# The order of the pieces in a program for linear attention and a feed-forward layer

## The chip, the cores and the metric

One core of one Trainium2 chip. The metric is the device time of one execution in microseconds (us). The kernel uses TensorE (PE in the profile), VectorE (DVE), ScalarE (ACT) and GpSimd (POOL) for arithmetic, and SyncE (SP) for most transfers. Each engine works through its own queue in the order in which the program gave its instructions out; an instruction that waits holds up all that stand behind it on that engine.

## The reference

```python
# q, k, v: (8, 8, 576, 64); w_in: (512, 2048); w_out: (2048, 512); all fp32
q_s = softmax(q, axis=-1)            # over the 64 of a head
k_s = softmax(k, axis=2)             # over the 576 positions
kv  = einsum('bhsd,bhse->bhde', k_s, v)   # per head k_s^T v, 64 x 64
x   = (q_s @ kv), heads side by side     # 4608 tokens x 512
g   = softplus(x @ w_in)             # 4608 x 2048
out = g @ w_out                      # 4608 x 512
```

q, k, v and w_in are drawn with large factors, so the products are done to nearly fp32 accuracy: each operand is split in a high part and a low rest, and a product is three matmuls (high x high, low x high, high x low).

## The kernel before, in words

The 4608 tokens are nine tiles of 512. The first three are done one by one: `U` makes one of 16 blocks of 128 of the hidden layer (12 matmuls, lines 595 to 597), `A` applies softplus on ScalarE (line 604), `G` or `H` splits the result in high and low parts (ScalarE line 610, VectorE line 613), `O` or `I` adds its product with a block of w_out (12 matmuls, lines 637 to 639), `F` stores the finished tile (line 653). The other six tiles are done as three pairs, with a scheme of seven products instead of eight on 2 x 2 blocks: `X` makes sums of the inputs (lines 679 to 686), `C` is a product of the first layer (lines 722 to 724, with evictions at 734 to 756), `t` a difference (803), `e` splits an operand in a high part (ScalarE, `e...0`, line 816) and a low part (VectorE, `e...1`, line 819), `d` is a product of the second layer (836 to 838), and `o` gathers and stores the pair's output: evictions on ScalarE (856) or VectorE (859), `flip` a transposition (873), `store` four stores on GpSimd's queue (881), and for the last block `addp`, `turnp`, `takep`, `storep` (889 to 905). In `C`, `d`, `e`, `t` and `o` the first number is the pair.

The scheme needs sums of weight blocks. `D` keeps a split weight in DRAM (line 220), `Y` and `y` make the sums (252 to 293) and their step 8 stores them in DRAM (265, 293), `R` and `r` fetch blocks and sums back (224 to 241, 790). Attention is made between the products: `n` loads keys and values (314 and 318, after GpSimd has cleared part of the buffer, 310 to 313), `k` makes kv of a head pair (336 to 413, products on PE at 387), `L` loads and `q` normalizes the queries (432, 453 to 502), and `x` multiplies them with kv (519 to 547, VectorE's low part at 529, products at 535 to 537). `l`, `T`, `M`, `S`, `J`, `P`, `Q` load, unpack, scale and split weights; `w` issues small matmuls that only keep PE running at the start (1038).

Nothing plans at run time. The string ORDER lists the tokens, and a loop at the end gives each token to `do`, which calls the piece of code that issues its instructions:

```python
        order = ORDER.split()
        for token in order:
            do(token)
```

Waits follow from the data: an instruction waits for its inputs, and for the buffer that it writes to be free. The pools have few buffers, so a load waits for the last reader of its buffer. A token `S` issues something only if its weight isn't in the set `signed` that `M` fills:

```python
                if at[0] not in signed:
                    sign_w(at[0], on(at, (nc.vector, nc.gpsimd, nc.scalar)))
```

Of the kernel before, what the change touches and what calls it, by code (L numbers as in the profile page):

```python
# [1096 lines left out]
```

## Time and profile before

| | before |
|---|---|
| time, median of 3 runs | 814.21 us (813.40 to 814.42) |
| profiled execution, span | 811.1 us; no time of its own is listed beside the span |
| median of the runs less that span | 3.1 us |
| PE busy | 800.8 us (99%) |
| VectorE, ScalarE, GpSimd busy | 625.9, 536.3, 115.1 us |
| transfers | 193.75 MB, mean 239 GB/s |

The span is the time from the first to the last recorded instruction; what lies around it is in the time of a run only. "SPq" is SyncE's queue of transfers, "PEld" the loading of weights into PE, which runs beside the matmuls. A matmul's record lasts longer than the distance to the next one, since matmuls are pipelined; the distance is the cost. A transfer has two times: that of its issue in a queue, and the time until it has landed.

### The profile page before, as it was taken

The page shows a single profiled execution, that of the slowest core. Times are in us where ns is not written, and L with a number is a line of the kernel's source. Part 1 is how long each engine was busy: PE and PEld are TensorE (multiplying, and loading weights), DVE is VectorE, ACT ScalarE, POOL GpSimd, SP SyncE. Part 2 cuts the span into 40 slices and gives each one's busy share as a digit, 9 for nine tenths or more (in the row PEclk, how much of TensorE's full clock was granted, in tenths as well). Part 3 has the DMA queues.
Part 4 walks back from the last instruction along what each step waited for, and adds up shares of the span by engine and source line. Part 5 has one row for each costly group of instructions (what it writes and reads, how often), then busy time and mean ns, then how long its engine had stood idle before and what let it go on. Part 6 is the DMA issues. An engine that isn't in the chain of part 4 may idle for free.

```text
span 811.1 us, 12147 instructions
## 1 busy us (share of the span) xinstructions
PE 800.8 (99%) x4244; PEld 656.6 (81%) x4244; DVE 625.9 (77%) x1027; ACT 536.3 (66%) x868; POOL 115.1 (14%) x219
## 2 busy tenths in 40 slices
...
GB/s 340 373 273 182 59 39 274 267 176 385 401 279 257 328 337 343 340 372 253 139 324 237 186 115 265 275 270 93 280 201 197 178 261 198 175 156 322 211 126 70
DMA packets 114493, 193.75 MB, mean 239 GB/s; under 512 B 8000, under 2 KB 90176, under 8 KB 104192
## 3 DMA queue, kind: packets, MB, share of 16 engines
...
## 4 chain that ended last, share of the span: by engine, by line
PE 92%; DVE 3%; issue 2%; DMA 2%; SPq 1%; ACT 0%; POOL 0%; DVEq 0%; ACTq 0%; POOLq 0%
PE po L722 6%; PE po L838 6%; PE po L836 6%; PE po L837 6%; PE po L724 6%; PE po L723 6%; PE ph L595 5%; PE po L637 5%; PE ph L597 5%; PE ph L596 5%; PE po L638 5%; PE po L639 5%; PE ph L722 3%; PE ph L724 3%; PE ph L723 3%; PE ph L836 3%
## 5 line engine op out<-in xcount | busy, mean ns | idle before, releaser
L881 POOL DMA_DIRECT2D out<-w x92 | 59.3, 653 | 305.7 <-DVE w L873 304.4
L816 ACT CAST g_hi<-w 128x512 fp32r<-128x512 f32 x74 | 46.2, 624 | 31.1 <-PE ph L837 8.0
L595 PE MATMUL ph<-x,w 128*128 128x512 f32 x164 | 65.3, 398 | 1.1 <-DMA w<-kept 1.1
L637 PE MATMUL po<-w,g_hi 128*128 128x512 f32 x164 | 64.5, 394 | 0.0
L596 PE MATMUL ph<-x,w 128*128 128x512 f32 x164 | 64.0, 390 | 0.0
L597 PE MATMUL ph<-x,w 128*128 128x512 f32 x164 | 64.0, 390 | 0.0
L639 PE MATMUL po<-w,g_lo 128*128 128x512 f32 x164 | 64.0, 390 | 0.0
L638 PE MATMUL po<-w,g_hi 128*128 128x512 f32 x164 | 63.9, 390 | 0.0
L819 DVE TENSOR_TENSOR g_lo<-w,g_hi 128x512 fp32r<-128x512 f32 x74 | 51.0, 690 | 16.0 <-ACT g_hi L816 12.6
L803 DVE TENSOR_TENSOR w<-w,w 128x512 f32<-128x512 f32 x72 | 49.2, 686 | 5.3 <-ACT w L756 5.2
L752 ACT ACTIVATE w<-w 128x512 f32<-128x512 f32 x48 | 30.1, 632 | 34.8 <-DVE w L745 18.9
L745 DVE TENSOR_TENSOR w<-po,w 128x512 f32<-128x512 f32 x24 | 16.6, 690 | 46.9 <-PE po L724 46.3
L816 ACT CAST w<-w 128x512 fp32r<-128x512 f32 x52 | 32.2, 623 | 25.1 <-DVE w L819 8.1
L604 ACT ACTIVATE g<-ph 128x512 f32<-128x512 f32 x48 | 28.6, 599 | 29.8 <-PE ph L597 26.7
L722 PE MATMUL po<-w,x 128*128 128x512 f32 x112 | 44.1, 394 | 0.0
L724 PE MATMUL po<-w,x 128*128 128x512 f32 x112 | 43.7, 390 | 0.0
L723 PE MATMUL po<-w,x 128*128 128x512 f32 x112 | 43.7, 390 | 0.0
L610 ACT CAST g_hi<-g 128x512 fp32r<-128x512 f32 x46 | 28.6, 621 | 21.2 <-PE po L638 20.7
L613 DVE TENSOR_TENSOR g_lo<-g,g_hi 128x512 fp32r<-128x512 f32 x46 | 31.4, 683 | 12.6 <-ACT g_hi L610 12.4
L339 POOL PARTITION_ALL_REDUCE mx<-mx x20 | 17.2, 860 | 160.6 <-DVE mx L336 133.0
L336 DVE TENSOR_REDUCE mx<-kvt 128x128 f32<-128x640 f32 x28 | 36.9, 1319 | 2.5 <-DMA kvt<-in_kv_tail 2.5
L819 DVE TENSOR_TENSOR w<-w,w 128x512 fp32r<-128x512 f32 x52 | 35.6, 689 | 3.1 <-ACT w L816 1.0
...
## 6 DMA issues: line engine op xcount, KB each, us to landing
...
```

What stands on the lines that cost most here:

```text
L595: nc.tensor.matmul(ph, lhsT=w_hi, rhs=x_hi, start=h == 0, stop=False)
L596: nc.tensor.matmul(ph, lhsT=w_lo, rhs=x_hi, start=False, stop=False)
L597: nc.tensor.matmul(ph, lhsT=w_hi, rhs=x_lo, start=False, stop=h == HP - 1)
L637: nc.tensor.matmul(po, lhsT=g_hi[:, ms], rhs=w_hi, start=j == 0, stop=False)
L638: nc.tensor.matmul(po, lhsT=g_hi[:, ms], rhs=w_lo, start=False, stop=False)
L639: nc.tensor.matmul(po, lhsT=g_lo[:, ms], rhs=w_hi, start=False, stop=j == NJ - 1)
L722: nc.tensor.matmul(ph, lhsT=w_hi, rhs=x_hi, start=c == 0 and i in (0, 4), stop=False, **more)
L723: nc.tensor.matmul(ph, lhsT=w_lo, rhs=x_hi, start=False, stop=False, **more)
L724: nc.tensor.matmul(ph, lhsT=w_hi, rhs=x_lo, start=False, stop=c == 1, **more)
L816: nc.scalar.copy(ring[p, i, s][0], right_of(p, i, s))
L819: engine.tensor_tensor(out=lo, in0=right_of(p, i, s), in1=hi.bitcast(F32), op=ALU.subtract)
L836: nc.tensor.matmul(bank, lhsT=w_hi, rhs=hi, start=begin, stop=False, **more)
```

## The change

ORDER is replaced by another list. It holds the same tokens, 2420 of the 2432; the 12 that are left out are `S` tokens of weights that are in `signed` at that point in the order before. No other line is changed. Of the diff, which replaces the whole list, five stretches are shown: the start, the end of the sum `Y1` of weight blocks, the stretch with the fetches of weight blocks 3 and 4, a stretch of the last pair, and the end. In each the removed lines are the old order from one token to another, and the added lines the new one; they are broken at other places here than in the file.

```diff
 ORDER = """
-    w0.20 b0 b1 q0.0 n k0.0.1 n q0.1 n n q0.2 q0.3 q0.4.1 l0 q0.5 l1 k0.0.2 k0.1.1 l2 k0.1.2 k0.0.3 k0.2.1
-    k0.0.4 k0.0.5 q0.6
+    w0.20 b0 q0.0 b1 q0.1 n n n n q0.2 q0.3 q0.5 q0.4.1 q0.6
...
-    Y1.7 k3.0.5 L4 H1.13.1 Y6.0 O28 k3.1.5 q3.0 A30 Y6.1 R0.1 q3.1 U31 H1.14.0 Y7.0 q3.12 H1.14.1 Y1.8
+    Y1.7 k3.1.4
...
-    k3.0.6 H1.15.0 y0.0 k3.1.6 q3.5 n H1.15.1 U32 k3.0.7 y0.1 k3.1.7 y0.2 q3.6 q3.7 R0.2 k3.0.8 O30 q3.8 A32
-    k3.0.9 y0.3 Y4.2 k3.1.8 n k3.2.0 U33 q3.13 k3.1.9 H2.0.0 q3.9 R0.3 H2.0.1 O31 k3.2.4 A33 q3.10 y1.0
-    k3.3.0 U34 F1.0 F1.1 q3.11 F1.2 F1.3 R0.4 k3.3.4 H2.1.0 U35 A34 H2.1.1 k3.2.5 y1.1 q4.0 O32 k3.3.5 q4.1
-    A35 y0.4 y1.2 y0.5 y1.3 q4.12 y2.0 k3.2.6 R0.5 y1.4 k3.3.6 H2.2.0 q4.2 n k3.2.7 q4.3 y0.6 O33 k3.2.8
-    H2.2.1 k3.3.7 k3.2.9 k3.3.8 q4.4 U36
+    k3.0.6 k3.1.5 n x2.3.5 k3.0.7 k3.0.8 k3.1.6 k3.1.7 k3.0.9 k3.1.8 k3.1.9 U32 q3.6 q4.1 q3.8 H1.15.0 O30 n
+    q3.5 q3.7 H1.15.1 O31 A32 U33 H2.0.0 q4.0 U34 Y1.8 H2.0.1 q3.13 R0.3 A33 H2.1.0 R0.4 F1.0 F1.1 Y7.1 y1.0
+    y0.0 F1.2 F1.3 O32 R0.5 U35 Y4.2 Y6.1 Y6.3 k3.2.0 k3.3.0 y0.1 y0.2 A34 y0.3 q3.9 y0.4 k3.3.4 y0.5 q4.12
+    k3.2.4 k3.2.5 k3.2.6 q3.10 H2.1.1 q4.2 q3.11 q4.3 k3.3.5 k3.3.6 k3.2.7 A35 H2.2.0 n U36
...
-    d2.2.7 e2.6.3.1 e2.4.2.0 e2.4.2.1 d2.4.0 t2.4.6 e2.4.3.0 r2.13 o2.c11.0 e2.4.3.1 d2.4.1 t2.4.7 e2.4.4.0
-    o2.c11.1 e2.4.4.1 d2.4.2 o2.flip.0.0 e2.4.5.0 e2.4.5.1 o2.store.0.0 d2.4.3
+    d2.2.7 e2.4.1.0 d2.4.0 r2.9 e2.4.1.1 d2.4.1 e2.4.3.0 e2.4.3.1 o1.store.1.1 e2.4.2.0 o2.c11.1 o2.flip.0.1
+    o2.c11.0 e2.4.2.1 d2.4.2 e2.4.4.0 e2.4.6.0 e2.4.4.1 t2.4.2 e2.6.0.0 e2.6.0.1 e2.4.5.0 d2.4.3
...
-    d2.5.7 e2.6.6.0 e2.6.6.1 d2.6.0.0 o2.c12.0 e2.6.7.0 d2.6.1.0 e2.6.7.1 d2.6.2.0 o2.c12.1 o2.flip.3.0
-    d2.6.3.0 d2.6.4.0 o2.flip.3.1 o2.store.3.0 d2.6.5.0 d2.6.6.0 d2.6.7.0 o2.store.3.1 d2.6.0.1 o2.c21.0
-    d2.6.1.1 o2.flip.2.0 d2.6.2.1 d2.6.3.1 o2.store.2.0 d2.6.4.1 d2.6.5.1 d2.6.6.1 d2.6.7.1 o2.addp.0
-    o2.addp.1 o2.turnp.0 o2.turnp.1 o2.takep.0 o2.turnp.2 o2.takep.1 o2.turnp.3 o2.takep.2 o2.storep.0
-    o2.takep.3 o2.storep.1
+    d2.5.7 o2.flip.0.0 e2.6.2.0 o2.store.0.0 e2.6.2.1 e2.6.1.1 d2.6.1.0 d2.6.0.1 e2.6.6.0 e2.6.6.1
+    o2.flip.1.1 d2.6.1.1 o2.store.1.1 o2.c12.1 d2.6.2.0 d2.6.2.1 o2.c12.0 o2.flip.3.0 r2.13 d2.6.3.0 d2.6.4.0
+    o2.store.3.0 o2.flip.3.1 e2.6.5.1 d2.6.5.0 o2.store.3.1 d2.6.6.0 e2.6.7.0 e2.6.7.1 d2.6.7.0 o2.c21.0
+    o2.flip.2.0 d2.6.3.1 d2.6.4.1 d2.6.5.1 d2.6.6.1 d2.6.7.1 o2.addp.0 o2.turnp.0 o2.takep.0 o2.addp.1
+    o2.turnp.1 o2.takep.1 o2.storep.0 o2.turnp.2 o2.takep.2 o2.turnp.3 o2.store.2.0 o2.takep.3 o2.storep.1
 """
```
## Rows read from the trace of the kernel before

**Rows 1.** The page's busy time: engine, us (share of the span) x instructions.
```profile
PE 800.8 (99%) x4244; PEld 656.6 (81%) x4244; DVE 625.9 (77%) x1027; ACT 536.3 (66%) x868; POOL 115.1 (14%) x219
```

**Rows 2.** The chain of work that ended last, shares of the span by engine.
```profile
PE 92%; DVE 3%; issue 2%; DMA 2%; SPq 1%; ACT 0%; POOL 0%; DVEq 0%; ACTq 0%; POOLq 0%
```

**Rows 3.** Who PE waited for: us in total, times, longest.
```profile
PE ph L595 <- DMA w<-kept: 1.1, 1, 1.1
...
PE att L535 <- DVE q_lo L529: 0.7, 1, 0.7
...
PE att L387 <- issue: 0.4, 1, 0.4
```

**Rows 4.** Windows: stretch, length, busy time of the engines, PEclk, DMA share, GB/s.
```profile
480.00:500.00 20.00, 19.87 (x88) 16.01 (x86) 17.43 (x29) 10.45 (x18) 5.47 (x8) 1.00 0.48 160
560.00:580.00 20.00, 20.00 (x90) 16.55 (x89) 15.71 (x25) 15.79 (x31) 0.00 (x0) 1.00 0.55 165
```

**Rows 5.** The chain of waits in order of time, around U35: start, us, what.
```profile
224.82 8.94 DMA w<-kept
...
233.89 0.47 PE ph L595
```

**Rows 6.** Timeline of SyncE's DMA queue, 208 to 232: start, duration, line, transfer.
```profile
208.98 0.76 SPq L265 DMA_DIRECT2D sums<-w  x1
...
218.57 0.55 SPq L314 DMA_DIRECT2D kvt<-in_kv  x1
219.17 1.73 SPq L318 DMA_DIRECT2D kvt<-in_kv_tail  x1
...
221.65 0.54 SPq L314 DMA_DIRECT2D kvt<-in_kv  x1
222.23 2.55 SPq L318 DMA_DIRECT2D kvt<-in_kv_tail  x1
224.82 0.85 SPq L224 DMA_DIRECT2D w<-kept  x1
...
231.14 1.43 SPq L224 DMA_DIRECT2D w<-kept  x1
```

**Rows 7.** Timeline, the products of two key/value units on PE.
```profile
217.60 1.39 PE L387 MATMUL att<-kvt 128*64 128x65 f32 x40
```

**Rows 8.** Line 265, the stores of the summed weights.
```profile
DMA to landing us min/median/max: 5.6/8.6/12.8
```

**Rows 9.** Line 224, the fetches of weight blocks.
```profile
DMA to landing us min/median/max: 4.7/8.3/10.6
```

**Rows 10.** Timeline around the short stall at 491.
```profile
489.80 0.62 ACT L816 CAST w<-w 128x512 fp32r<-128x512 f32 x1
...
490.70 0.69 DVE L819 TENSOR_TENSOR w<-w,w 128x512 fp32r<-128x512 f32 x1
490.92 0.39 PE L837 MATMUL po<-w,spare 128*128 128x512 f32 x1
...
491.44 0.51 PE L838 MATMUL po<-w,spare 128*128 128x512 f32 x1
```

**Rows 11.** The page's costliest groups: busy us, mean ns of one, idle before.
```profile
L816 ACT CAST g_hi<-w 128x512 fp32r<-128x512 f32 x74 | 46.2, 624 | 31.1 <-PE ph L837 8.0
...
L819 DVE TENSOR_TENSOR g_lo<-w,g_hi 128x512 fp32r<-128x512 f32 x74 | 51.0, 690 | 16.0 <-ACT g_hi L816 12.6
```

**Rows 12.** Groups by line: the eviction of line 856.
```profile
L856 ACT ACTIVATE w<-po 128x512 f32<-128x512 f32 x17 | 10.1, 592 | 8.3 <-PE po L838 8.1
```

**Rows 13.** The chain of waits at the start.
```profile
23.84 1.76 PE ph L1038 x14
25.60 3.44 PE po L558 x8
```

**Rows 14.** Timeline of GpSimd near the end.
```profile
797.94 7.69 POOL L881 DMA_DIRECT2D out<-w  x12 [5.00 <-DVE w L873]
```

**Rows 15.** Timeline of SyncE's DMA queue at the end.
```profile
807.49 1.21 SPq L904 DMA_DIRECT2D out<-w  x2
```

**Rows 16.** Line 881, GpSimd's stores of the result.
```profile
DMA to landing us min/median/max: 2.2/2.9/6.5
```

More of the change, by code (lines that the diff above doesn't have):

```diff
@@ new lines @@
+    w0.20 b0 q0.0 b1 q0.1 n n n n q0.2 q0.3 q0.5 q0.4.1 q0.6 k0.0.1 k0.0.2 k0.1.1 k0.0.3 k0.1.2 k0.2.1 k0.2.2
+    k0.1.3 w5.5 k0.2.3 k0.0.4 k0.0.5 k0.1.4 k0.1.5 k0.2.4 k0.2.5 k0.3.1 k0.3.2 k0.0.6 l0 T0 M0.1 w1.6 l1 l2 l3 n
+    l4 q0.8 k0.3.3 q0.7 k0.1.6 k0.3.4 z1 T1 M1.1 k0.3.5 k0.0.7 k0.0.8 q0.12 q0.13 q0.9 w2.3 q0.11.1 w3.2 w4.2
+    q0.10 T2 k0.1.7 k0.1.8 k0.2.6 k0.3.6 k0.2.7 k0.2.8 x0.1.0 x0.1.1 T3 x0.0.0 x0.0.1 x0.2.0 x0.2.1 n k0.3.7
+    k0.3.8 x0.3.0 x0.1.2 l5.6.7.8.9 J0 x0.3.1 x0.0.2 B0 L1 k1.0.0 k1.0.1 B1 x0.2.2 B2 x0.3.2 k1.0.2 M3 S3.1 J1
@@ new lines @@
+    k1.0.3 k1.0.4 B3 k1.1.0 x0.1.3 x0.1.4 T4 M4.1 U0 M2.1 J2 k1.0.5 J3 U1 A0 P2 Q2 k1.1.1 x0.2.3 k1.1.2 x0.0.3
+    A1 x0.0.4 x0.3.3 x0.3.4 k1.0.6 k1.0.7 T5 P3 x0.2.4 Q3 T7 O0 U2 U3 M5 A2 J4 P4 Q4 G2 k1.1.3 A3 O1 O2 S5.1 J5
+    k1.1.4 M7.1 q1.0 q1.1 q1.2 T6 q1.3 P5 M6.1 J7 W1 Q5.1 U4 k1.1.5 G3 T8 J6 M8.1 J8 A4 U5 A5 k1.1.6 P6 Q6 G4 D6
+    q1.4 T9 M9 O3 O4 P7 Q7 U6 U7 G5 k1.1.7 z0 k1.0.8 O5 P8 Q8 S9 J9 T12 A6 U8 T10 G6 O6 M10 S10 J10 T11 D7
+    k1.1.8 P9 Q9 k1.2.0 T15 A7 P10 k1.0.9 k1.2.1 G7 D5 O7 k1.3.0 k1.1.9 k1.3.1 k1.2.2 T13 k1.2.3 k1.2.4 U9 A8
@@ new lines @@
+    Q10 U10 q1.6 G8 T14 O8 M12.1 M11.1 J11 k1.2.5 J12 W2 P11 W0 k1.3.2 k1.3.3 Q11 M13.1 k1.3.4 A9 A10 k1.2.6
+    k1.2.7 P12 Q12 J13 G9 M15.1 J15 U11 U12 q1.8 O9 k1.3.5 k1.3.6 M14.1 G10 O10 J14 q1.5 q1.7 P13 Q13 A11 A12
+    G11 O11 U13 k1.2.8 k1.2.9 k1.3.7 G12 P14 Q14 P15 q1.9 q1.10 x1.0.0 Q15.1 U14 q1.11 A13 k1.3.8 k1.3.9 x1.1.0
+    O12 P0 W3 x1.0.1 x1.0.2 x1.0.3 G13 A14 G14 x1.0.4 x1.0.5 O13 x1.1.1 x1.1.2 x1.1.3 U15 x1.2.0 x1.2.1 x1.2.2
+    x1.1.4 x1.2.3 O14 Q0.1 x1.1.5 P1 Q1.1 D1 x1.3.0 x1.3.1 x1.3.2 x1.3.3 L2 A15 x1.2.4 x1.2.5 D15 x1.3.4 x1.3.5
@@ new lines @@
+    H1.7.0 H1.7.1 n A24 H1.8.0 U25 k2.3.6 O23 D10 D12 k3.0.0 Y4.0 H1.8.1 L3 Y4.1 D13 x2.0.1 U26 x2.0.2 Y2.3
+    x2.0.3 A25 H1.9.0 q3.1 Y3.2 Y3.3 H1.9.1 Y3.4 k2.3.7 A26 Y2.4 k2.3.8 O24 O25 Y2.5 Y2.6 k2.3.9 Y3.5 Y3.6 Y2.7
+    x2.1.0 x2.1.1 H1.10.0 Y1.0 Y1.2 Y1.3 x2.0.4 U27 A27 H1.10.1 D8 x2.0.5 x2.2.0 k3.0.4 k3.0.5 x2.1.2 U28 A28
+    Y1.4 n x2.1.3 x2.1.4 H1.11.0 x2.2.1 Y1.5 Y1.6 q3.0 U29 q3.12 x2.1.5 x2.3.0 Y2.8 R0.0 D9 O26 H1.12.0 Y0.5
+    H1.11.1 O27 x2.2.2 x2.2.3 Y3.7 A29 Y3.8 L4 R0.1 H1.13.0 Y6.0 U30 H1.12.1 O28 A30 Y6.2 k3.1.0 U31 Y7.0 Y7.2
@@ new lines @@
+    H1.13.1 q3.2 q3.3 q3.4 x2.3.1 Y0.6 x2.2.4 Y0.7 Y0.8 A31 x2.3.2 H1.14.0 x2.3.3 R0.2 O29 Y1.7 k3.1.4 H1.14.1
+    x2.3.4 x2.2.5 k3.0.6 k3.1.5 n x2.3.5 k3.0.7 k3.0.8 k3.1.6 k3.1.7 k3.0.9 k3.1.8 k3.1.9 U32 q3.6 q4.1 q3.8
+    H1.15.0 O30 n q3.5 q3.7 H1.15.1 O31 A32 U33 H2.0.0 q4.0 U34 Y1.8 H2.0.1 q3.13 R0.3 A33 H2.1.0 R0.4 F1.0 F1.1
+    Y7.1 y1.0 y0.0 F1.2 F1.3 O32 R0.5 U35 Y4.2 Y6.1 Y6.3 k3.2.0 k3.3.0 y0.1 y0.2 A34 y0.3 q3.9 y0.4 k3.3.4 y0.5
+    q4.12 k3.2.4 k3.2.5 k3.2.6 q3.10 H2.1.1 q4.2 q3.11 q4.3 k3.3.5 k3.3.6 k3.2.7 A35 H2.2.0 n U36 Y7.3 q4.4
@@ new lines @@
+    k3.2.8 k3.2.9 x3.0.0 y0.6 n q4.5 O33 U37 H2.2.1 O34 R0.6 R0.7 k3.3.7 y1.1 H2.3.0 H2.3.1 k4.0.0 q4.6 q4.8
+    R2.0 x3.0.1 x3.0.2 x3.0.3 k3.3.8 k3.3.9 x3.1.0 k4.1.0 A36 H2.4.0 O35 y2.0 x3.1.1 x3.1.2 x3.1.3 Y4.3 Y4.4
+    x3.0.6 A37 x3.2.0 Y7.4 R0.8 U38 H2.5.0 x3.2.1 q4.7 H2.4.1 x3.2.2 x3.2.3 k4.0.4 q4.13 Y5.1 k4.0.5 y0.7 Y7.5
+    y0.8 q4.9 O36 x3.1.6 x3.3.0 H2.5.1 x3.2.6 y2.1 k4.0.6 y1.2 y1.3 x3.3.1 x3.3.2 A38 H2.6.0 Y4.5 q4.11 k4.1.4
+    k4.1.5 O37 n x3.3.3 x3.3.6 U39 A39 H2.7.0 R0.9 k4.0.7 R0.10 y1.4 y3.1 Y6.4 q4.10 k4.1.6 k4.0.8 k4.2.0 y3.0
@@ new lines @@
+    U40 U41 y1.5 y1.6 k4.2.4 H2.6.1 H2.7.1 O38 O39 Y7.6 y4.0 y3.2 Y6.5 y1.7 k4.1.7 A40 n y4.1 Y5.0 Y4.6 Y6.6
+    H2.8.0 H2.8.1 O40 k4.1.8 Y6.7 A41 H2.9.0 k4.2.5 y2.2 k4.3.0 k4.0.9 H2.9.1 Y4.7 k4.3.4 k4.3.5 Y7.7 U42 A42
+    k4.1.9 y1.8 y4.2 Y5.2 k4.2.6 k4.2.7 y2.3 R0.11 k4.2.8 y5.0 Y5.3 Y5.4 k4.3.6 k4.3.7 k4.3.8 Y4.8 X0.1.hB11
+    k4.2.9 y3.3 x4.0.0 x4.0.1 O41 y3.4 y3.5 Y5.5 R0.12 H2.10.0 Y5.6 U43 R0.13 A43 Y7.8 x4.0.2 Y6.8 H2.10.1
+    k4.3.9 x4.1.0 x4.0.3 x4.1.1 x4.1.2 U44 x4.1.3 Y5.7 H2.11.0 x4.0.6 x4.2.0 Y5.8 X0.0.hB11 X0.0.lB11 x4.2.1
@@ new lines @@
+    x4.2.2 x4.1.6 A44 O42 H2.12.0 x4.3.0 x4.2.3 x4.3.1 H2.11.1 O43 X0.0.T1 X0.0.hT1 R0.14 R0.15 y5.1 R3.1.0
+    x4.3.2 x4.2.6 X0.0.hB22 X0.0.T3 x4.3.3 X0.0.lB22 X0.0.T2 y4.3 n n R3.0.0 y3.6 H2.12.1 x4.3.6 X0.0.hB21
+    X0.0.lB21 y2.4 X0.1.lB11 X0.1.T1 X0.1.T3 X0.1.hT1 y4.4 X0.1.hB22 X0.1.lB22 X0.1.T2 y2.5 U45 U46 A45 A46
+    X0.1.hB21 X0.1.lB21 X0.1.hT3 O44 X0.0.T4 H2.13.0 U47 H2.14.0 X0.1.hT2 X0.1.T4 y4.5 y5.2 y4.6 R2.1 X0.0.hT2
+    H2.13.1 H2.14.1 y6.0 R4.1.0 y3.7 O45 y3.8 y6.1 y7.1 y5.3 y5.4 y7.0 X0.0.hT3 X0.1.hT4 X0.1.lT4 R4.3.0 A47
@@ new lines @@
+    C0.0.0 C0.0.7 y4.7 y6.2 y2.6 X0.0.hT4 H2.15.0 I2.14.1 I2.14.0 H2.15.1 X0.0.lT4 C0.0.2 y4.8 I2.15.1 y5.5 y5.6
+    I2.15.0 X0.1.lT1 X0.0.lT1 L5 F2.0 X0.1.lT2 X0.0.lT2 C0.0.1 C0.0.8 C0.1.0 F2.1 y5.7 y6.3 y6.4 y6.5 C0.0.3
+    R4.0.0 R3.2.0 C0.1.7 C0.1.2 C0.1.1 C0.0.10 X0.0.lT3 F2.2 C0.0.5 y7.2 F2.3 X0.1.lT3 C0.0.4 C0.0.11 q5.1 y2.7
+    C0.1.8 k5.0.0 y7.3 y7.4 k5.0.4 y7.5 C0.1.3 C0.0.9 e0.0.0.0 C0.2.0 e0.0.0.1 C0.0.6 C0.1.10 k5.1.0 y5.8
+    C0.0.14 C0.1.4 C0.1.11 C0.2.7 y7.6 C0.2.2 R2.2 C0.1.5 C0.2.1 R3.3.0 C0.1.6 C0.2.9 k5.1.4 C0.1.9 k5.0.5 q5.0
@@ new lines @@
+    k5.3.7 C0.3.6 C0.3.15 C0.4.5 R2.6 C0.5.7 C0.5.2 C0.6.0 k5.2.8 k5.2.9 x5.0.0 x5.0.1 R4.7.0 C0.4.14 C0.6.7
+    C0.5.1 C0.5.8 k5.3.8 x5.0.2 x5.0.3 C0.4.11 C0.4.6 y7.7 C0.0.16 C0.5.3 q6.0 k5.3.9 x5.0.6 t0.1.0 C0.5.10
+    x5.1.0 x5.1.1 q6.1 q6.12 x5.1.2 C0.2.12 C0.4.12 C0.5.4 k6.0.0 C0.5.5 C0.5.11 k6.1.0 x5.1.3 R3.7.0 C0.5.14
+    C0.5.9 C0.6.1 C0.6.8 x5.2.0 x5.2.1 x5.1.6 R4.5.0 C0.5.6 C0.7.0 C0.6.3 x5.2.2 x5.2.3 y7.8 C0.5.15 k6.0.4
+    C0.6.2 k6.0.5 x5.2.6 C0.6.10 k6.1.4 C0.7.7 x5.3.0 k6.0.6 R4.6.0 R2.7 C0.7.1 t0.1.3 C0.4.15 x5.3.1 e0.0.1.0
@@ new lines @@
+    e0.0.1.1 k6.1.5 x5.3.2 C0.6.4 e0.0.2.0 x5.3.3 e0.0.3.0 C0.6.11 C0.6.12 t0.1.4 C0.2.16 n k6.0.7 k6.0.8 k6.0.9
+    k6.2.0 C0.6.5 C0.6.14 r0.0 e0.0.2.1 C0.7.4 C0.6.6 C0.6.15 k6.2.4 x5.3.6 k6.1.6 k6.1.7 n C0.7.8 t0.1.1
+    C0.1.12 C0.6.9 k6.1.8 k6.1.9 X1.0.hB11 C0.7.2 C0.7.9 C0.7.3 C0.7.10 q6.2 q6.3 d0.0.0 d0.0.1 r0.1 q6.4 q6.6
+    d0.0.2 X1.1.hB11 e0.0.6.0 C0.7.11 e0.0.3.1 k6.3.0 C0.7.6 e0.0.4.0 e0.0.5.0 r0.4 C0.7.5 r0.2 t0.1.5 q6.5
+    k6.2.5 k6.3.4 k6.3.5 C0.7.15 C0.7.16 e0.0.4.1 q6.7 d0.0.3 q6.8 k6.2.6 C0.7.12 k6.2.7 k6.3.6 e0.0.5.1
@@ new lines @@
+    e0.1.2.1 t0.3.2 n d0.1.2 t0.2.7 d0.1.3 r0.9 e0.1.4.0 t0.2.5 t0.3.0 C0.5.16 X1.0.hB21 e0.1.6.0 t0.3.4
+    e0.1.4.1 d0.1.4 e0.1.5.0 e0.2.0.0 e0.1.5.1 e0.1.6.1 e0.1.7.0 X1.1.lB11 o0.v.1 d0.1.5 d0.1.6 e0.1.7.1 d0.1.7
+    e0.2.1.0 e0.2.0.1 C0.3.16 d0.2.0 X1.1.lB21 t0.3.5 n t0.3.7 e0.2.2.0 e0.2.2.1 e0.2.3.0 e0.2.1.1 d0.2.1 t0.4.3
+    e0.2.3.1 C0.4.16 e0.2.4.0 e0.2.5.0 e0.2.4.1 o0.u.1 d0.2.2 d0.2.3 e0.2.7.0 q6.9 q6.10 k6.3.9 e0.2.5.1 t0.4.7
+    C0.6.16 x6.0.0 e0.2.6.0 e0.2.6.1 x6.0.1 e0.2.7.1 d0.2.4 x6.1.0 e0.4.0.0 d0.2.5 d0.2.6 e0.4.1.0 e0.4.0.1
@@ new lines @@
+    e0.4.1.1 x6.0.2 e0.4.2.0 t0.4.4 o0.u.0 e0.4.2.1 t0.3.6 d0.2.7 e0.4.3.0 r0.8 q6.11 d0.4.0 e0.4.3.1 x6.0.3
+    x6.0.6 x6.1.1 x6.1.2 d0.4.1 d0.4.2 e0.4.4.0 e0.4.4.1 x6.2.0 X1.0.lB11 x6.1.3 e0.4.5.0 e0.4.5.1 x6.2.1 x6.1.6
+    X1.1.T1 r0.13 d0.4.3 e0.4.7.0 d0.4.4 e0.4.6.0 e0.4.6.1 e0.5.0.0 d0.4.5 r0.12 o0.v.0 x6.2.2 x6.2.3 r0.10
+    x6.2.6 x6.3.0 x6.3.1 d0.4.6 e0.5.2.0 t0.4.0 e0.4.7.1 d0.4.7 e0.5.1.0 X1.0.T1 x6.3.2 e0.5.0.1 o0.c22.1 d0.5.0
+    e0.5.1.1 d0.5.1 e0.5.4.0 e0.5.5.0 e0.5.3.0 X1.0.T3 X1.0.hB22 e0.5.2.1 o0.c22.0 e0.5.3.1 e0.5.4.1 d0.5.2
@@ new lines @@
+    o0.c11.0 e0.5.6.0 x6.3.3 d0.5.3 d0.5.4 x6.3.6 R3.0.1 C1.0.0 X1.0.lB22 X1.0.T2 e0.5.5.1 X1.1.hB22 d0.5.5
+    X1.1.T3 t0.4.2 X1.1.lB22 X1.1.T2 e0.5.6.1 X1.1.T4 X1.1.hT2 d0.5.6 R2.8 e0.6.0.0 e0.6.1.0 e0.6.0.1 e0.6.1.1
+    R3.1.1 e0.5.7.0 e0.5.7.1 d0.6.0 X1.0.hT1 d0.5.7 t0.4.6 o0.c11.1 C1.0.7 X1.0.lB21 X1.0.T4 C1.0.2 t0.4.5
+    d0.6.1 X1.0.lT1 e0.6.3.0 e0.6.2.0 e0.6.2.1 d0.6.2 e0.6.4.0 e0.6.5.0 X1.0.hT2 e0.6.3.1 e0.6.6.0 d0.6.3
+    e0.6.7.0 R2.9 X1.0.hT4 R3.2.1 X1.0.lT2 e0.6.4.1 d0.6.4 e0.6.5.1 X1.1.lT2 o0.flip.0.1 C1.0.1 e0.6.6.1 d0.6.5
```

89 lines of the change are left out of this document (88 added, 1 removed).

## The prediction, made before the change was run

> **What bounds the kernel now.** I read the share of busy time first. PE is busy 99% of the 811.1 us span [rows 1], and the chain that ended last is 92% PE [rows 2], so an order can pay only where PE stands still. A quiet stretch shows what PE does otherwise: 90 matmuls in 20 us, all of it busy, clock 1.00 [rows 4], one about every 0.227 us, so a product of six takes 1.36 us. The list of waits, PE as the waiter, is what an order can remove: 1.1 us at line 595 for a weight block still on its way from DRAM, 0.7 us at line 535 for VectorE's `q_lo`, 0.4 us at line 387 [rows 3]. The timeline adds one that the list leaves out: near 491 us the step from one matmul to the next is 0.52 us, where its neighbours take 0.23, so 0.29 us is lost [rows 10]; the window that holds it is 19.87 us busy of 20 [rows 4]. Together 1.1 + 0.7 + 0.4 + 0.3 = 2.5 us is all that another order can give back, 0.3% of the time.
>
> The largest has a clear cause. SyncE's queue issued block 3 at 224.82, and U35 could start only when it had landed, at 233.89 [rows 5]. It went out late because two key/value loads stand ahead of it on SyncE (218.57 to 224.78 with a fetch between them), and these wait for the products that free their buffers, which PE runs from 217.60 [rows 6, 7].
>
> **The change, part by part.** All instructions stay: the 12 `S` tokens that go issued nothing (the `signed` set already held their weights). So PE's 4244 matmuls and their duration stay, and nothing is saved on PE but waits. I count each wait's place in the new order by the products that lie between the step that releases a value and the step that uses it, and compare with the durations of what lies between on the other engines.
>
> *Fetch of block 3 (the 1.1 us).* In the new order the release is k3.0.6, k3.1.6 and U35 is six 12-matmul steps after them instead of five (one such step is 12 x 0.227 = 2.73 us). PE frees the first buffer at about 218.3, as before, and would reach U35 at 218.3 + 0.7 + 6 x 2.73 = 235.4. SyncE has two loads ahead (2.3 and 3.1 us with their tails, [rows 6]) and the store Y1.8 (0.76), so block 3 leaves at about 224.8 again; with its 8.94 us [rows 5] it is there at 233.8. This stall goes: -1.1.
>
> *Fetch of block 4, the next in line.* What was ahead is now on the path. Before, the store Y1.8 (whose staging buffer block 4 is fetched into) was issued at 208.98, long before R0.4 at 231.14 [rows 6]. Now Y1.8 stands behind the two loads, at about 224.1, and R0.4 behind Y1.8; SyncE waits there until the store has landed. Stores of this line took 5.6, 8.6 and 12.8 us (least, median, most) [rows 8], fetches 4.7, 8.3 and 10.6 [rows 9]. By medians: 224.1 + 8.6 + 8.3 = 241.0. U36 comes after seven 12-matmul steps and the key products k3.1, k3.2 and k3.3 (each 0.7, half of the 1.39 of [rows 7]): 218.3 + 19.1 + 2.1 = 239.5. So U36 is 1.5 us late; bounds 0 (least values: 234.4) and 8.0 (most: 247.5). I take the medians, rounded down: +1.4. Behind R0.4 on SyncE stand four output stores, R0.5 and the next loads; U37 comes 5.4 us after U36, and moves with it.
>
> [...]
>
> *The 0.7 us at line 535 and the 0.4 us at line 387.* Both waiting steps stand behind other matmuls in the new order, and VectorE's work ahead of them is issued earlier. I count them as gone; -1.1. If not, the sum is up to 1.1 higher.
>
> *The 0.3 us at 491.* A chain of a cast on ScalarE and a subtraction on VectorE, both in queue behind other work (489.80 to 491.39, [rows 10]). In the new order this pair has more room: -0.3.
>
> *New tight places.* In the `C` and `d` stages the new order often leaves one product (1.36 us) between the step that frees or feeds and the step that needs. I laid the durations of [rows 11, 12] (0.62 cast, 0.69 subtraction, 0.59 eviction, neighbours overlapping by some 0.1) into these gaps. Seven chains keep under 0.45 us: o0.c22.1 to e0.5.1.1 0.15, X0.0.lT2 before C0.0.1 0.25, C2.0.11 before X2.0.lT4 0.28, k3.1.7 before H1.15.1 0.31, e0.4.2.0 before o0.u.0 and e2.5.2.0 before o2.v.0 0.34 each, C1.7.15 before e1.0.6.1 0.40. The durations hide something: a matmul ends 0.39 us after its start and the next starts 0.23 after it [rows 10], so 0.16 of the gap is not there, and each hand-over takes some 0.05 (491.39 to 491.44). With 0.3 hidden, three are late by 0.2 in all; if each is as late as the one in [rows 10], 7 x 0.29 = 2.0. I take that price for the three tightest: +0.9.
>
> *The order of preparation.* Before, the pairs `e` (cast and subtraction) stand in the order in which `d` uses them, but for 4 places; now 30 neighbouring pairs are exchanged. Where the staging slots turn over, an early pair that waits for a slot holds up the one needed first. The worst I found: ScalarE has e2.4.3.0, e2.4.2.0, c11.1 and VectorE then flip.0.1 and e2.4.2.1 before d2.4.2, all starting from the end of d2.2.7: 0.62 + 0.62 + 0.59 + 0.69 + 0.69 = 3.2, less 0.3 of overlap, plus 0.16 and 0.15 of hand-overs, against two products, 2.7. Late by 0 to 0.8; I take +0.5. The others have two or more products more.
>
> *Start and end.* At the start a query maximum moves ahead, and three groups of filler matmuls stand before the third and fourth head's products; counted by hand the first x products still begin near 25.6 [rows 13]. Bounds -0.7 and +0.7, taken at 0. At the end flip.2.0 moves behind d2.6.7.0, and GpSimd issues five groups of four stores from about 794.5 on (17 half products of 0.68 before PE's end), 0.64 each as in [rows 14]: 794.5 + 12.8 = 807.3, plus 2.9 to land [rows 16] is 810.2. SyncE's last stores leave by 808.7 [rows 15] and end the span at 811.1. GpSimd stays just under: 0, with +1 if one flip is late. ScalarE's changed order of functions loads a table two times less; ScalarE is not the bound, so nothing.
>
> Sum: -1.1 - 1.1 - 0.3 + 1.4 + 0.9 + 0.5 = +0.3. It is against the profiled execution's span, 811.1, which lies 3.1 us under the median of the runs, 814.21; the same 3.1 around it gives 814.5.
>
> **The rivals.** *Faster: the covers hold.* The store and the fetch for U36 land like the faster half (together under 15.4 us), and the tight places lose what 0.3 hidden says: -2.5 + 0.2 + 0.2 = -2.1, so 812.1, and 811.0 if the start gains too. For it: by the same count the order of before has chains with 0.6 us to spare too, and only one stall of this kind [rows 10]. Against: the transfers around U36 follow each other closely [rows 6].
>
> *Slower: the store-to-fetch chain.* Y1.8 then R0.4 take over 18 us, which is 1.5 above the medians and well under their most (23.4); SyncE holds everything behind R0.4 for as long, so R0.5 and the loads of k4 come late too. Price: 3 to 5 us at U36, with the rest of the sum at -1.1 (the +1.4 left out): 816.1 to 818.1. It decides from where landing passes 15.4 us, and beats the return of 2.5 from 17.9 us on.
>
> *Slower: the exchanged pairs.* If each of the 30 exchanges costs 0.1 to 0.2 us, because a slot's release passes three engines, that is 3 to 6 us in many small steps between 350 and 800: 816 to 820. Against it: most have two products or more of cover.
>
> *It does nothing.* PE's matmuls are 99% of the time and all stay; the stalls move by a step and come back at the next late block. 814.2. This falls in with the forecast.
>
> **How the numbers follow.** A difference under 0.2%, 1.6 us, is about what a measurement of this kernel can't tell from none. Forecast with the case of no effect 0.40 (its own range 812.6 to 815.8); faster 0.31, within it about 811.6; the store-to-fetch chain 0.15; the exchanged pairs 0.14. So faster 0.31, same 0.40, slower 0.29. The range, 811.0 to 818.6, leaves out the ends of the outer cases, about one in ten on either side.
>
> **What would show it.** Right: the wait at line 595 is gone at U35 and one of 1 to 2 us stands one step later, R0.4 waiting on Y1.8 in SyncE's queue; no wait at lines 535 and 387; a gap of half a us before d2.4.2 near 775. Wrong: U36 without a wait (then faster), or PE's busy share in the windows from 350 to 800 falling below 19.8 of 20 in several (then slower), or GpSimd's stores ending the span.

## The result, and the profile after

The changed kernel takes 820.14 us (median of 4, 819.78 to 822.42), the kernel before 814.3 beside it: a ratio of 1.0079, with an interval of 1.0064 to 1.0095. It is slower by 5.8 us. In a second set of executions it was 818.31 (816.79 to 820.58) against 813.57, 1.0054 (1.0038 to 1.0069); why the two differ is told with the ninth run. The profiled execution has a span of 817.7 us, 6.6 more than before. Lines after ORDER have numbers higher by 157: line 529 of before is 686 here, 502 is 659, 207 is 364, 595 is 752, 185 is 342, 194 is 351. In the kernels of runs 1 to 8 and 10 these numbers are 3 lower again (686 is 683 there).

First the page's share of PE and the chain, as in [rows 1, 2]:

```profile
PE 806.0 (99%) x4244; PEld 659.6 (81%) x4244; DVE 632.7 (77%) x1027; ACT 523.3 (64%) x866; POOL 113.0 (14%) x219
```
```profile
PE 95%; DVE 2%; DMA 1%; issue 0%; SPq 0%; ACT 0%; DVEq 0%
```

The same 4244 matmuls are busy 5.2 us longer: busy time itself grew, which waits alone don't do. What PE waited for, as in [rows 3]:

```profile
PE ph L1195 <- DVE ident L277: 3.0, 1, 3.0
PE att L692 <- DVE q_lo L686: 2.9, 1, 2.9
PE ph L740 <- DVE w L351: 0.9, 1, 0.9
PE att L544 <- issue: 0.7, 1, 0.7
```

The wait for weight block 3 is gone, as forecast, and none has come in its place at U36. But at the line whose wait the prediction counted as gone, PE waits 2.9 us for `q_lo`, instead of 0.7, and at another place: near 118, where before it was near 256. The windows around it (columns as in [rows 4]):

```profile
100.00:110.00 10.00, 10.00 (x62) 8.06 (x61) 8.65 (x17) 6.66 (x11) 2.05 (x4) 1.00 0.21 61
...
115.00:118.20 3.20, 0.31 (x2) 0.00 (x0) 3.02 (x7) 0.62 (x1) 0.00 (x0) 0.90 0.00 0
118.20:124.20 6.00, 5.99 (x16) 4.99 (x17) 3.08 (x5) 1.07 (x2) 0.00 (x0) 0.50 0.00 0
124.20:130.00 5.80, 5.80 (x30) 4.97 (x30) 2.02 (x3) 2.58 (x4) 1.99 (x1) 0.98 0.00 0
```

PE stands still for 2.9 of 3.2 us, and in the 6 us after it the granted clock is 0.50: 16 matmuls, where run 8 has 30 in the same window. These 6 us count as busy. What they cost shows beside runs 8 and 10 (below), where the clock stayed at 1.00 behind the same wait: from the product that had waited to the key products near 147 the same work takes 29.1 us here (118.21 to 147.33) and 26.3 there (117.62 to 143.91, 117.88 to 144.13), so 2.8 us. One place costs 2.9 + 2.8 = 5.7 us of the 6.6. The timeline of VectorE and GpSimd before it:

```profile
108.42 2.42 POOL L364 TENSOR_TENSOR w<-w,w 128x1024 fp32r<-128x1024 f32 x1 [6.21 <-ACT w L362]
...
108.89 3.03 DVE L659 TENSOR_TENSOR qt<-qt,s 128x1024 f32<-128x1024 f32 x1
...
111.95 0.73 DVE L676 STREAM_TRANSPOSE att<-qt 128x512 f32<-128x512 f32 x1
...
112.25 2.44 POOL L364 TENSOR_TENSOR w<-w,w 128x1024 fp32r<-128x1024 f32 x1 [1.41 <-ACT w L362]
...
112.59 3.19 DVE L659 TENSOR_TENSOR qt<-qt,s 128x1024 f32<-128x1024 f32 x1
...
117.47 0.69 DVE L686 TENSOR_TENSOR q_lo<-att,q_hi 128x512 fp32r<-128x512 f32 x1
...
118.21 0.42 PE L692 MATMUL att<-q_hi,kv_hi 128*128 128x64 f32 x1 [2.90 <-DVE q_lo L686]
```

The two multiplications of line 659 last 3.03 and 3.19 us; the median of that line is 1.22. Each begins while GpSimd subtracts (line 364), and ends 1.1 us after GpSimd has ended (108.42 + 2.42 = 110.84, end 111.92; 112.25 + 2.44 = 114.69, end 115.78), nearly the 1.22 us that it takes alone. Together they cost VectorE 1.8 + 2.0 = 3.8 us, and `q_lo` is late. Before, the same pieces met otherwise; this is the trace of the kernel before, VectorE and GpSimd:

```profile
115.22 2.45 POOL L207 TENSOR_TENSOR w<-w,w 128x1024 fp32r<-128x1024 f32 x1 [28.62 <-ACT w L205]
...
116.27 0.69 DVE L529 TENSOR_TENSOR q_lo<-att,q_hi 128x512 fp32r<-128x512 f32 x1 [0.66 <-ACT q_hi L525]
...
127.65 1.22 DVE L467 TENSOR_TENSOR qt<-qt,m 128x1024 f32<-128x1024 f32 x1
127.69 2.96 POOL L467 TENSOR_TENSOR qt<-qt,m 128x1024 f32<-128x1024 f32 x1 [0.99 <-DVE m L464]
```

In the first pair VectorE's subtraction lies wholly within GpSimd's and takes 0.69 us, the median of its line; of its two inputs `att` lies in PSUM. In the second VectorE began 0.04 us earlier and kept its 1.22; GpSimd took 2.96, where its other instruction of this line took 1.91 us. In these pairs, but for the first, the one that began first kept its time and the other took 1.0 to 2.0 us longer. A third kind of pair in the changed kernel is like them: a VectorE subtraction with both inputs in SBUF (line 770, at 150.12), of 0.68 us else, lasts 2.11 beside a GpSimd subtraction (line 624) that began 0.36 us before it; PE doesn't wait there. A copy of VectorE with one input (line 597, at 53.44), of 0.19 us else, lasts 2.22 beside GpSimd's line 364 as well. Which instructions of VectorE are lengthened, and whether PSUM is what spares the first pair, no run shows.

At the start the same thing happens once more, between a scaling on GpSimd and a joining on VectorE of 1.22 us else:

```profile
30.77 2.52 POOL L342 TENSOR_SCALAR w<-w 128x1024 bf16<-128x1024 f32 x1 [4.49 <-ACT w L323]
30.78 3.31 DVE L351 SCALAR_TENSOR_TENSOR w<-w 128x1024 uint32<-128x1024 uint32 x1
...
34.15 3.71 PE L740 MATMUL ph<-x,w 128*128 128x512 f32 x8 [0.91 <-DVE w L351]
```

GpSimd is 0.01 us earlier, and PE's wait of 0.9 us follows. The first product of O0 begins at 38.63; it was at 36.97 before. But 1.2 of these 1.7 us lie ahead of everything that the order moves, in the small matmuls of `w0.20` (40 records) that open both kernels, here before and after:

```profile
2.99 6.07 PE L1038 MATMUL ph<-ident 128*128 128x128 f32 x40 [2.99 <-DVE ident L120]
2.99 7.26 PE L1195 MATMUL ph<-ident 128*128 128x128 f32 x40 [2.99 <-DVE ident L277]
```

The trace's first record of a granted clock of 1.00 begins 5.8 us into the span before and 8.3 us into it here. That goes with the execution and not with the order: the 40 records take 6.99 us in run 9's profile of this same kernel, and 6.07 (run 1) to 7.17 (run 6) in those of the other runs, which begin with the same tokens. From the next matmul on it is 27.99 us to O0 before (8.98 to 36.97) and 28.45 here (10.18 to 38.63), so the new start itself is 0.5 us longer.

### The profile page after: what moved, and what is told of

It is laid out like the page before. It is cut to its first block, busy times and chain, and to the rows that moved or that the text cites. A ratio compares the mean times of both kernels' runs of the same rounds, so it can differ in the third digit from the quotient of the medians.

```text
span 817.7 us, 12034 instructions
## 1 busy us (share of the span) xinstructions
PE 806.0 (99%) x4244; PEld 659.6 (81%) x4244; DVE 632.7 (77%) x1027; ACT 523.3 (64%) x866; POOL 113.0 (14%) x219
## 4 chain that ended last, share of the span: by engine, by line
PE 95%; DVE 2%; DMA 1%; issue 0%; SPq 0%; ACT 0%; DVEq 0%
PE po L993 7%; PE po L995 7%; PE po L994 7%; PE po L879 6%; PE po L881 6%; PE po L880 6%; PE po L794 5%; PE ph L752 5%; PE po L796 5%; PE po L795 5%; PE ph L754 5%; PE ph L753 5%; PE ph L879 3%; PE ph L880 3%; PE ph L881 3%; PE ph L993 3%
## 5 line engine op out<-in xcount | busy, mean ns | idle before, releaser
L794 PE MATMUL po<-w,g_hi 128*128 128x512 f32 x164 | 65.8, 402 | 0.0
L795 PE MATMUL po<-w,g_hi 128*128 128x512 f32 x164 | 64.6, 394 | 0.0
L796 PEld LDWEIGHTS po<-w,g_lo 128*128 128x128 f32 x164 | 31.2, 190 | 7.5 <-DVE g_lo L770 0.7
```

The source lines that it names most:

```text
L794: nc.tensor.matmul(po, lhsT=g_hi[:, ms], rhs=w_hi, start=j == 0, stop=False)
L795: nc.tensor.matmul(po, lhsT=g_hi[:, ms], rhs=w_lo, start=False, stop=False)
L796: nc.tensor.matmul(po, lhsT=g_lo[:, ms], rhs=w_hi, start=False, stop=j == NJ - 1)
```

## The experiments

Each is the changed kernel with an edit of its order; the times of before beside them were 813.6, 813.8 and 813.6 in the three sets (runs 1 to 4, 5 to 8, 9 and 10). Each set ran on another chip, so a time is best read against the kernel before of its own set: the changed kernel lay 5.8 us above it in the first executions, and 4.7 in run 9.

**1. VectorE does the two subtractions.**

```diff
- ... P15 q1.9 q1.10 x1.0.0 Q15.1 U14 q1.11 ... O14 Q0.1 x1.1.5 ...
+ ... P15 q1.9 q1.10 x1.0.0 Q15 U14 q1.11 ... O14 Q0 x1.1.5 ...
```

> The changed order, with the two subtractions of weight blocks 15 and 0 (1.23 us each on VectorE, 2.43 on GpSimd) given to VectorE at the same place in its queue, so that GpSimd is idle near 108 to 116 us. Theory A (VectorE and GpSimd lock each other out: the query multiplications last 3.0 and 3.2 us instead of 1.22 only because GpSimd's subtraction runs): both are 1.22 again, VectorE reaches q_lo some 2.5 us earlier although it does more, PE's wait of 2.9 us falls to about 0.5, the clock stays at 1.00, and the time falls from 820.1 by 5 to 6 us, to 814 to 815. Theory B (VectorE simply has too much queued ahead of q_lo in the new order): VectorE has 1.2 us more ahead of q_lo, the wait grows to about 4 us, and the time rises to 821 or more.

814.42 us, 1.0008 (0.9999 to 1.0017). Its trace, VectorE and the product:

```profile
106.95 1.23 DVE L656 TENSOR_TENSOR qt<-qt,s 128x1024 f32<-128x1024 f32 x1
108.21 0.73 DVE L673 STREAM_TRANSPOSE att<-qt 128x512 f32<-128x512 f32 x1
108.84 1.20 DVE L361 TENSOR_TENSOR w<-w,w 128x1024 fp32r<-128x1024 f32 x1
109.97 1.20 DVE L656 TENSOR_TENSOR qt<-qt,s 128x1024 f32<-128x1024 f32 x1
...
113.59 0.30 PE L689 MATMUL att<-q_hi,kv_hi 128*128 128x64 f32 x1 [0.23 <-DVE q_lo L683]
```

VectorE does one subtraction more ahead of `q_lo` and is done sooner; both multiplications are back at 1.2. PE's wait is 0.23, 2.7 us less: the 3.8 us by which the two multiplications were longer, less the 1.1 of the subtraction (108.84 to 109.97). Theory A holds, B falls: 0.8 us over the kernel before are left of 5.8. Not all of this need be the edit's doing. At the start, which the edit leaves alone, VectorE's joining began first in this profile, and kept its time:

```profile
30.00 1.26 DVE L348 SCALAR_TENSOR_TENSOR w<-w 128x1024 uint32<-128x1024 uint32 x1
30.22 3.44 POOL L339 TENSOR_SCALAR w<-w 128x1024 bf16<-128x1024 f32 x1 [4.88 <-ACT w L320]
```

It is 27.68 us to O0 from the first 40 records on, for 28.45 in the changed kernel. Which way the start went in the other ten executions isn't known. Run 6 has the start as in the changed kernel.

**2. Small matmuls in the wait.** An added token `f24` ahead of x1.0.3:

```diff
+            elif kind == "f":
+                ps = bank_h()
+                for _ in range(at[0]):
+                    nc.tensor.matmul(ps[:, 0:P], lhsT=ident, rhs=ident, start=True, stop=True)
```

> The changed order, with 24 small matmuls (0.11 us each, 2.7 us) on PE in front of the product that waits for q_lo; their result is not read. Theory C (the slow matmuls from 118.2 to 124.2, granted clock 0.50, follow from PE's idle time just before, and are half of the loss): PE no longer idles, the clock stays at 1.00, the wait itself costs the same 3 us, and the time falls by about 3 us, to 817. Theory D (the slow stretch has another cause, or PE can be fed no faster there): the clock still falls to 0.50, or the time stays within 0.5 us of 820.1.

820.09 us, 1.0082. The time tells nothing: each of them is two matmuls in the trace, 48 records and 5.5 us, so they ended 2.3 us after `q_lo` was ready and took away what the clock gave back. The clock does tell: its mean is 0.999 or 1.0 in all five executions, and 0.995 to 0.997 in all five of run 3 on the same chip, where PE stands still for 2.9 us at this place. So the fall comes with PE's standing still.

**3. The start.**

```diff
- ... B2 x0.3.2 k1.0.2 M3 S3.1 J1 k1.0.3 k1.0.4 B3 k1.1.0 x0.1.3 x0.1.4 T4 ...
+ ... B2 x0.3.2 k1.0.2 J1 k1.0.3 k1.0.4 B3 k1.1.0 x0.1.3 M3 S3.1 x0.1.4 T4 ...
```

> The changed order, with the scaling and signing of weight block 3 (ScalarE, then 2.5 us on GpSimd) moved a few tokens later near 30 us, so that VectorE's joining of block 1 starts before GpSimd and lasts 1.22 instead of 3.31 us. Theory A: PE's wait of 0.9 us at line 740 near 34 us goes, and what is done at 30 to 60 us comes 0.9 to 1.5 us earlier: 818.6 to 819.2. Theory B (the start is bounded by what VectorE has to do in all): no change beyond 0.4 us, 819.7 to 820.5.

818.21 us, 1.0063 (1.0049 to 1.0077): 1.9 less than in the first set, but against the kernel before 4.6 instead of 5.8, 1.2 less, which the two intervals don't separate. The trace tells more. VectorE begins first and keeps its time, GpSimd waits for it:

```profile
29.95 1.22 DVE L348 SCALAR_TENSOR_TENSOR w<-w 128x1024 uint32<-128x1024 uint32 x1
30.47 3.10 POOL L339 TENSOR_SCALAR w<-w 128x1024 bf16<-128x1024 f32 x1 [5.02 <-ACT w L320]
31.38 4.46 PE L737 MATMUL ph<-x,w 128*128 128x512 f32 x10
...
36.61 3.87 PE L787 MATMUL po<-w,g 128*128 128x512 f32 x8
```

O0 begins at 36.61 instead of 38.63; 1.0 of these 2.0 us lies in the first 40 records (6.23 instead of 7.26), and 1.0 behind them (27.45 us to O0 for 28.45). The edit moves ScalarE's part of this weight too, and that part wasn't tried alone; in run 1's profile, without this edit, VectorE's going first was worth 0.8.

**4. Both edits.**

> The edits of the first and the third of these runs together. Theory A: the gains add, 820.1 - 5.5 - 1.2 = 813.4, with 812.6 to 814.2, so at or a little under the kernel before. If the two hide each other (a shift of the start also shifts what meets near 115 us), 814 to 816.

813.4 us, 0.9998 (0.999 to 1.0007). Against the kernel before beside them, run 1 takes 5.0 of the 5.8 us away, run 3 1.2, and both edits 6.0: the gains add, and the kernel is back at the time of before.

**5. Half as many fillers.** `f12` instead of `f24`.

> The fillers of the run before took 0.22 us each, not 0.11, and ended 2.3 us after q_lo was ready, so its time doesn't tell. Now 12 of them, 2.6 us, which end before q_lo is ready near 117.7. Theory C (the slow stretch of 6 us follows from PE's idle time and costs some 3 us): clock 1.00 throughout, time 817.0 to 817.8. Theory D (PE loses nothing by the clock): 819.8 to 820.4.

817.03 us, 1.0043 (1.0029 to 1.0056). The windows after the wait:

```profile
115.00:118.20 3.20, 2.98 (x27) 2.79 (x26) 3.02 (x7) 0.33 (x1) 0.00 (x0) 1.00 0.00 0
118.20:124.20 6.00, 6.00 (x30) 5.12 (x30) 3.65 (x7) 2.73 (x5) 0.00 (x0) 1.00 0.00 0
```

`q_lo` is as late as before, PE is kept busy meanwhile, and 30 matmuls run where 16 ran. In all six executions the mean clock is 0.999 or 1.0, and the time is 3.2 us over before instead of 5.8: as long as the executions of the changed kernel whose clock stayed (816.79 to 817.71 in run 9). On this chip the changed order ran without fillers only in the one execution of run 8, and its clock stayed too, so that PE's standing still brings the fall rests on runs 2 and 3. The execution profiled here took 819.55 us, the slowest of the six, with a wait of 1.3 us for a weight block at line 876: a time near 820 alone doesn't tell of the clock.

**6. One subtraction of the two.** `Q0.1` becomes `Q0`, `Q15.1` stays.

> The changed order, with only the second of the two subtractions (weight block 0) given to VectorE; GpSimd keeps that of block 15, which meets the first query multiplication. Theory A: the first multiplication lasts 3.0 us as before, the second 1.22 instead of 3.19, so q_lo comes 2 us earlier, PE's wait falls from 2.9 to about 1 us; whether the clock falls after a wait of 1 us is open: 816.0 if it stays, up to 818 if it falls. Theory B (the length of VectorE's queue): 819 or more, and both multiplications longer than 2 us.

815.05 us, 1.0015 (1.0005 to 1.0025), 1.2 us over before instead of 5.8. The first multiplication lasts 3.05 us, the second 1.20; the wait is 0.9 us, and the clock stays at 1.00 behind it:

```profile
108.72 3.05 DVE L656 TENSOR_TENSOR qt<-qt,s 128x1024 f32<-128x1024 f32 x1
...
112.44 1.20 DVE L656 TENSOR_TENSOR qt<-qt,s 128x1024 f32<-128x1024 f32 x1
...
116.05 0.30 PE L689 MATMUL att<-q_hi,kv_hi 128*128 128x64 f32 x1 [0.90 <-DVE q_lo L683]
```

**7. The other waits taken out too.** Run 4, and four moves more:

```diff
- q1.11 A13 k1.3.8 k1.3.9 x1.1.0 O12 P0 W3 x1.0.1 x1.0.2 x1.0.3
+ q1.11 W3 x1.0.1 x1.0.2 A13 k1.3.8 k1.3.9 x1.1.0 O12 P0 x1.0.3
...
- y0.3 q3.9 y0.4 k3.3.4 y0.5 q4.12 k3.2.4 k3.2.5 k3.2.6
+ y0.3 q3.9 k3.2.4 k3.2.5 y0.4 k3.3.4 y0.5 q4.12 k3.2.6
...
- H2.9.1 Y4.7 k4.3.4 k4.3.5 Y7.7
+ H2.9.1 k4.3.4 k4.3.5 Y4.7 Y7.7
...
- C1.4.3 e1.0.1.1 C1.5.7 C1.5.1 x7.0.0 x7.0.1 x7.0.2 x7.0.3
+ C1.4.3 C1.5.7 C1.5.1 x7.0.0 x7.0.1 x7.0.2 e1.0.1.1 x7.0.3
```

> The run with both edits, and four waits more that its trace shows taken out by moving VectorE's tokens: x1.0.2 ahead of k1.3.9 and x1.1.0 (0.4 us near 113), k3.2.4 and k3.2.5 ahead of two sums of weights (0.85 near 238), k4.3.4 ahead of Y4.7 (0.3 near 287), e1.0.1.1 behind x7.0.2 (0.3 to 0.6 near 541). If the waits add to the time one by one: 813.4 - 1.9 = 811.5, with 811.0 to 812.2, so faster than the kernel before (813.6) by some 2 us. If each only moves the wait to the next late step: 813 to 813.6.

811.84 us (810.63 to 813.62) against 813.84, 0.9978 (0.9967 to 0.9989): faster than both kernels, by 2.0 us against before. PE's list of waits is down to three:

```profile
PE ph L1192 <- DVE ident L274: 3.0, 1, 3.0
PE po L1050 <- DVE w L1043: 0.5, 1, 0.5
PE ph L876 <- DMA x<-sums: 0.3, 1, 0.3
```

Only the one for the identity matrix at the very start is long; it is 3.0 us in every profile here.

**8. A narrower chain.**

```diff
- o0.c22.1 d0.5.0 e0.5.1.1 ... e0.5.2.1 o0.c22.0 e0.5.3.1
+ o0.c22.1 o0.c22.0 d0.5.0 e0.5.1.1 ... e0.5.2.1 e0.5.3.1
```

> The changed order, with the eviction o0.c22.0 (0.69 us on VectorE) moved between o0.c22.1 and e0.5.1.1, the chain that the prediction gave 0.15 us of room. The trace of the changed order shows no stall there, and in it the low part made by e0.5.1.1 is read first by the third matmul of its product, 0.46 us after the first. If the room is counted to the third matmul (0.3 us were left: 476.83 to 477.16), the product's third matmul comes 0.3 to 0.4 us late; if to the first, with the prediction's 0.3 us of hidden time, 0.7 us or more late; nothing if the eviction overlaps more than the rows show. No time of the whole kernel is to be told from this.

One execution, for its trace at the place:

```profile
472.12 1.29 DVE L1013 SCALAR_TENSOR_TENSOR w<-po,w 128x512 f32<-128x512 f32 x2 [0.40 <-PE po L992]
...
473.28 0.39 PE L990 MATMUL po<-g_hi,x 128*128 128x512 f32 x1
...
473.32 0.68 DVE L973 TENSOR_TENSOR g_lo<-w,g_hi 128x512 fp32r<-128x512 f32 x1
473.51 0.39 PE L991 MATMUL po<-g_hi,x 128*128 128x512 f32 x1
...
474.06 0.50 PE L992 MATMUL po<-g_lo,x 128*128 128x512 f32 x1 [0.17 <-DVE g_lo L973]
```

The first two matmuls of the product (`g_hi`) start on time, at 473.28 and 473.51; the third, which reads `g_lo`, starts at 474.06 instead of 473.74, 0.32 us late. The room is to be counted to the third matmul.

**9 and 10. The changed kernel and the narrower chain again.** In run 8 the wait of 2.9 us was as in the changed kernel, but the clock after it was 1.00 and the time 817.0.

> The changed kernel as it is, once more. In its first profile and in that of the run with the start mended, PE's clock fell to 0.50 for 6 us after the wait of 2.9 us; in the profile of the run with the narrowed chain, the same wait of 2.9 us left the clock at 1.00 and the time was 817.0. If the fall belongs to this program's order, it is there again: mean clock 0.995 to 0.997 in every execution, 820 us. If it depends on the chip or the execution, some executions have a mean clock of 0.999 and 817 us.

> The narrowed chain once more, on the same chip as the changed kernel. It differs from it by one eviction near 475 us, so what PE does up to 120 us is the same. If the fall of the clock belongs to the execution or the chip, its times spread as those of the changed kernel do, 817 or 820 by the mean clock (0.999 or 0.996), with 0.3 us more for the late matmul. If it belongs to the program, all are near 817.

Both spread. The changed kernel: 816.79, 816.88 and 817.71 us with a mean clock of 0.999 to 1.0, and 818.9, 819.55 and 820.58 with 0.995 to 0.997. The narrower chain: 817.64 with 0.999, and 818.62 to 821.23 with 0.995 to 0.998. So the wait is there in every profile of this order, and the fall of the clock behind it in some executions: by the mean clock in all four of the first set and three of six here, 2.7 us between the medians of the latter. Two of run 10 (820.03 and 820.43, mean 0.998) can't be sorted by it, since executions of the kernel before show 0.998 too. The narrower chain's profile of this set, windows after the same wait:

```profile
115.00:118.20 3.20, 0.33 (x3) 0.33 (x3) 3.02 (x7) 0.47 (x1) 0.00 (x0) 1.00 0.00 0
118.20:124.20 6.00, 6.00 (x31) 5.15 (x31) 3.68 (x7) 2.64 (x5) 0.00 (x0) 1.00 0.00 0
```

Up to there the two programs do the same on PE. What decides whether the clock falls isn't shown. In the changed kernel's first profile the record of a granted 1.00 that begins at 8.3 ends 109.2 us later, at 117.6, 2.2 us into the wait (115.3 to 118.2). In run 9's the clock is 0.81 from 115.0 to 118.2 and 0.53 from there to 124.2, so there too the fall begins before the wait has ended. In runs 8 and 10 both windows show 1.00. No run moved the wait alone against the clock's record.

## Why the prediction was wrong

The forecast was +0.3 us and a range to 818.6; measured was +5.8. The forecast's positive terms are none of them in the trace; what made the time longer is not in the forecast. That the executions of run 9 whose clock stayed lie inside the range is luck: their wait of 2.9 us has no term either.

*The step that failed* is the one on the wait at line 535: "VectorE's work ahead of them is issued earlier. I count them as gone; -1.1. If not, the sum is up to 1.1 higher." I took the durations of VectorE's instructions from the trace of before as if they went with the instruction. Here they went with what GpSimd does beside it: in the new order two query multiplications begin behind GpSimd's subtractions and last 1.8 and 2.0 us longer; instead of 0.7 us the line waits 2.9. The old wait did go, as counted; the bound of 1.1 had no room for a new one at the same line. Runs 1, 4 and 6 show it by giving the subtractions to VectorE, one or both: PE's wait falls to 0.2 (run 1) and 0.9 us (run 6), and the time to 0.8 and 1.2 us over before instead of 5.8. That an instruction of VectorE or GpSimd can last longer beside one of the other stood in no rival, though the trace of before had a pair to see it in (127.69, 2.96 against 1.91 us).

*The clock* had no term. I read 1.00 in the windows of before, where the longest wait after the start was 1.1 us. Behind the wait of 2.9 us it was 0.50 for 6 us in the first profile: 2.8 us more by the traces of runs 8 and 10, 2.7 by the times of run 9; that it comes with PE's standing still is by runs 2 and 3. With 0.9 us of wait (run 6) it stayed.

*The start*, taken at 0 with bounds of 0.7, was +1.7 at O0 (38.63 for 36.97), of which 1.2 are the first 40 records, so the execution's, and 0.5 the order's. Two things stand behind the 0.5. The wait of 0.7 us at line 350 of before, which the prediction's list of waits leaves out, is gone; and the joining beside GpSimd takes 0.8 to 1.2 back, by the profiles of runs 1, 3, 4 and 7, where VectorE begins first and O0 comes 27.3 to 27.7 us behind the 40 records. I had counted orders there, not who stands beside whom.

*Weight block 3*, -1.1: right. *Block 4*, +1.4: wrong. The loads ahead took SyncE 3.0 us, from 226.53 to 229.52, not 5.5 as in [rows 6]; the store took 7.3 instead of the median 8.6, and the fetches of that stretch 5.4 to 10.2 us. This is SyncE's queue:

```profile
229.58 0.58 SPq L422 DMA_DIRECT2D sums<-w  x1
230.20 7.04 SPq L381 DMA_DIRECT2D w<-kept  x2
```

The second fetch leaves when the store has landed, at 236.9, as said, and U36 starts at 248.49 without a wait for it, after 11.6 us, where the prediction's sum left 6.8. The mechanism is there and decides nothing. U36 without a wait was the prediction's sign of a faster kernel; it came, and the loss came from elsewhere.

*The wait at line 387*, counted as gone, is 0.7 us now, near 246. *The one at 491* is gone.

*The tight places*, +0.9: none. None of the seven is among PE's waits, and for the one that it narrows run 8 shows why: the low part is read by a product's third matmul, 0.46 us after the first, so chains that end in a low part have that much more room than I counted. [Rows 10] could have told it: the matmul that came late there is L838, the third. Why the others of the seven (to `o0.u.0`, say) cost no wait isn't shown.

*The exchanged pairs*, +0.5: none; PE is busy 20.00 of 20 us in each window from 740 to 800, and no wait there is on its list. *The end*: no change, 0.5 us of wait before the transpositions as before.

By the spans: 2.9 (wait) + 2.8 (clock) + 1.2 (the first 40 records) + 0.5 (start) - 1.1 (block 3) - 0.7 (`q_lo` near 256) - 0.3 (491) + 0.3 (line 387) = 5.6 of the 6.6; the other 1.0 I did not follow up.
